# Another table for the order of all operations, and ten corrected costs of the plan, in a one-core attention and feed-forward kernel

## The chip, the core and the metric

The kernel runs on one core of a Trainium2 chip. The metric is the device time of one execution in microseconds (us); lower is better. A core has five engines that work side by side and meet through semaphores: PE (TensorE: matrix products into PSUM), DVE (VectorE), ACT (ScalarE), POOL (GpSimd) and SP (SyncE, which here issues every DMA). Each engine takes its instructions strictly in the order in which the program holds them, so an instruction that waits holds up all that stand behind it on the same engine.

## The reference

Inputs are `q`, `k`, `v` of 8 batches x 8 heads x 576 tokens x 64, a threshold `tau`, and the weights `w_in` (512 x 2048) and `w_out` (2048 x 512), all wanted in float32 precision.

```python
scores = (q @ k.transpose(0, 1, 3, 2)) / 8
thresh = scores.max(-1) - tau
scores = where(scores >= thresh, scores, -1e9)
attn   = exp(scores - scores.max(-1));  attn /= attn.sum(-1) + 1e-9
x      = heads joined(attn @ v)                  # 4608 tokens x 512
h      = x @ w_in
g      = where(h >= 1, h, where(h <= -1, 0, (h + 1)**2 / 4))
out    = g @ w_out                               # 4608 x 512
```

## The kernel before

Products run in float16 with each number split in a high and a low part (three products instead of one); the scores of batch 0 alone run in float32. The work is cut into 4921 operations, each an engine, an assumed cost in us, and a function that issues its instructions.

- **Weights.** 16 tiles of `w_in` and 16 of `w_out` are loaded (line 792), joined from their two halves (ACT L806 and L815, POOL L813, DVE L821 and L823), squared and summed on PE (`gram`, L834) to find a scale (`w_scale`: DVE L741, PE L744, DVE L481 to L483 and L749), then scaled and split in two parts (POOL L878 to L890, ACT L876 and L882, DVE `rest2` L893, or on PE `diff` L896/L897 and `scaled` L906).
- **q and k** of batch 0 are loaded straight into the tiles `qq` and `kk` (`load32`, L572). Those of later batches go to `raw` (L588), are squared (ACT L594), summed on PE (`sums`, L602, three or four very small products), turned into a scale (DVE `pow2` L481 to L483 and `scales` L610), and split (DVE L634 among others). **v** is loaded to `raw` (L658).
- **Attention.** A tile is 128 query rows of a head. PE makes the scores (`qk32` L1015 for batch 0, `qk` L1026 after that) into one of two PSUM buffers `s`; DVE takes the largest (L1078; for some tiles it copies the scores to a `raw` buffer as well and so frees `s` at once), ACT the exponential (L1087), DVE masks and sums (L1104, or L1091 from a `raw` copy, L1131 for a few), a reciprocal (L1112 or L1116), POOL scales (L1119), ACT and POOL split (L1125, L1128), SP transposes by DMA (L1144), and PE multiplies with v (`av`, L1245). ACT L1253 and DVE L1257 write the result into the buffers `x`.
- **Feed-forward.** `ffn1` (PE L1336) multiplies an `x` block with `w_in`; ACT L1342 and L1345, DVE L1349, ACT L1353 and DVE L1357 make the two parts of g; `ffn2` (PE L1379) multiplies with `w_out` into `acc`; ACT L1397 moves it to `ob`, SP stores it (L1404).

What sets the order: `Plan.order()` goes through the operations in the order of the table `ORDER` (lines 38 to 234, 4921 numbers), gives each a buffer and a start by the assumed costs, sorts all operations by that start, and issues them in that sequence. So the table and the costs together fix the order on every engine and which buffer each operation takes; the instructions themselves are the same for any table.

```python
for o in (self.ops[n] for n in ORDER):
    t = max(o.t, idle[o.eng], dma - self.QUEUE if o.eng == "SP" else 0.0)
    ...
return sorted((self.ops[n] for n in ORDER), key=lambda o: o.t)
```

Of the kernel before, what the change touches and what calls it, by code (L numbers as in the profile page):

```python
# [369 lines left out]
def attn_ffn_kernel(ctx: ExitStack, tc: tile.TileContext, qT, kT, vT, tau, w_in, w_out, out):  # L370
# [7 lines left out]
    B, H, D, S = qT.shape  # L378
# [134 lines left out]
    def tau_consts():  # L513
        V.tensor_scalar(tcs[:, 0:1], tau_sb, 0.0, 2.0 ** -51, ALU.is_ge, ALU.mult)
        V.tensor_scalar(tcs[:, 2:3], tau_sb, 0.0, None, ALU.max)
        V.tensor_scalar(tcs[:, 3:4], tau_sb, 0.0, -(D ** -0.5), ALU.is_ge, ALU.mult)

    c_op = plan.op("POOL", 5.7, consts)
    plan.op("ACT", 0.49, warm_up, [c_op])
    t_ld = plan.op("SP", 0.45, lambda: Y.dma_start(tau_sb, tau.broadcast_to([P, 1])), work=LOAD)  # L520
    t_op = plan.op("DVE", 0.56, tau_consts, [t_ld])
# [919 lines left out]
```

## Time and profile before

| | |
|---|---|
| three timed runs | 1104.99, 1105.64, 1106.31 us; median 1105.64 |
| profiled execution, first to last instruction | 1103.6 us (its time by the clock of the timed runs isn't given) |
| PE busy | 1064.5 us (96%), 9825 matmuls |
| DVE busy | 866.3 us (78%) |
| ACT busy | 840.9 us (76%) |
| POOL busy | 778.9 us (71%) |
| mean granted PE clock | 0.987 |

Busy shares are means over the whole span. In the page's 40 slices of 27.6 us, PE's busy tenths read 6, 7, 6, 8 and then 9 to the end, while DVE reads 6 and then 9 in the next five. A wait that the profile names is the idle time of an engine just before an instruction and what ended it.

### The profile page before, as it was taken

The page shows a single profiled execution, that of the slowest core. Times are in us where ns is not written, and L with a number is a line of the kernel's source. Part 1 is how long each engine was busy: PE and PEld are TensorE (multiplying, and loading weights), DVE is VectorE, ACT ScalarE, POOL GpSimd, SP SyncE. Part 2 cuts the span into 40 slices and gives each one's busy share as a digit, 9 for nine tenths or more (in the row PEclk, how much of TensorE's full clock was granted, in tenths as well). Part 3 has the DMA queues.
Part 4 walks back from the last instruction along what each step waited for, and adds up shares of the span by engine and source line. Part 5 has one row for each costly group of instructions (what it writes and reads, how often), then busy time and mean ns, then how long its engine had stood idle before and what let it go on. Part 6 is the DMA issues. An engine that isn't in the chain of part 4 may idle for free.

```text
span 1103.6 us, 26734 instructions
## 1 busy us (share of the span) xinstructions
PE 1064.5 (96%) x9825; PEld 716.7 (65%) x9825; DVE 866.3 (78%) x2379; ACT 840.9 (76%) x1522; POOL 778.9 (71%) x951
## 2 busy tenths in 40 slices
PE   6768899999999999999999999999999999999998
PEld 4557547665776666766666676766676666666674
DVE  6999998888888888888788787778687788876432
ACT  6888769798887787878778778877777787676443
POOL 6899998779878897778667677777666667466000
PEclk9799999999999999999999999999999999999999
DMA  9996688778985986587856776786657657645300
GB/s 330 303 289 117 136 158 163 122 143 162 184 136 113 174 154 122 121 176 146 164 107 108 152 154 124 129 146 124 146 91 130 138 113 127 118 80 113 72 1 29
DMA packets 419316, 154.91 MB, mean 140 GB/s; under 512 B 398193, under 2 KB 398193, under 8 KB 419185
## 3 DMA queue, kind: packets, MB, share of 16 engines
q1 hardware_dynamic: 419184, 153.21, 68.5%
q8 instruction: 77, 1.26, 0.5%
q14 instruction: 55, 0.44, 0.1%
HBM read 45.09 MB, written 9.44 MB: 49 GB/s over the span
## 4 chain that ended last, share of the span: by engine, by line
PE 80%; DVE 4%; POOL 2%; ACT 1%; issue 1%; DVEq 0%; POOLq 0%; ACTq 0%
PE ph L1336 31%; PE acc L1379 31%; PE s L1026 9%; PE ph L1245 9%; DVE e L1104 1%; DVE s L1078 1%; POOL e L1119 1%; ACT e L1087 0%; POOL hl L1128 0%; DVE kk L634 0%; DVE halves L1357 0%; DVE halves L893 0%; DVE vb L690 0%; DVE e L1091 0%; DVE qq L634 0%
## 5 line engine op out<-in xcount | busy, mean ns | idle before, releaser
L1128 POOL TENSOR_TENSOR hl<-e,hl 128x576 f16<-128x576 f32 x280 | 362.3, 1299 | 89.9 <-ACT hl L1125 81.1
L1336 PE MATMUL ph<-x,halves 128*128 128x256 f16 (+1 forms) x4032 | 400.0, 258 | 3.5 <-DVE halves L821 1.8
L1379 PE MATMUL acc<-halves 128*128 128x512 f16 x1728 | 398.0, 379 | 1.6 <-DVE halves L912 1.5
L1336 PEld LDWEIGHTS <-halves 128*128 128x128 f16 x4032 | 345.0, 98 | 62.5 <-issue 17.6
L1379 PEld LDWEIGHTS <-halves 128*128 128x128 f16 x1728 | 161.1, 98 | 189.3 <-issue 19.1
L1119 POOL TENSOR_SCALAR e<-e,sm 128x576 f32<-128x576 f32 x280 | 221.5, 797 | 70.6 <-DVE sm L1112 53.4
L1087 ACT ACTIVATE e<-s,sm 128x576 f32<-128x576 f32 x273 | 198.4, 739 | 87.9 <-DVE s L1078 67.3
L1078 DVE TENSOR_SCALAR_CACHE_REDUCE s<-s,pc 128x576 f32<-128x576 f32 x252 | 199.0, 821 | 80.2 <-PE s L1026 79.8
L1104 DVE SCALAR_TENSOR_TENSOR e<-s,sm,e 128x578 f32<-128x578 f32 x265 | 212.7, 815 | 38.5 <-ACT e L1087 22.0
L1125 ACT ACTIVATE hl<-e 128x576 f16<-128x576 f32 x280 | 187.8, 679 | 39.2 <-POOL e L1119 29.9
L1342 ACT ACTIVATE asq<-ph,fcs 128x512 f32<-128x512 f32 (+1 forms) x160 | 115.5, 734 | 44.7 <-PE ph L1336 42.4
L1349 DVE SCALAR_TENSOR_TENSOR ph<-ph,fcs,asq 128x512 f32<-128x512 f32 (+1 forms) x160 | 111.6, 699 | 42.0 <-ACT asq L1345 41.0
L1357 DVE SCALAR_TENSOR_TENSOR halves<-ph,fcs,halves 128x512 f16<-128x512 f32 (+1 forms) x192 | 112.8, 610 | 18.3 <-ACT halves L1353 17.6
L1245 PE MATMUL ph<-eT,vst 128*64 128x320 f16 (+2 forms) x1928 | 123.5, 283 | 2.5 <-DVE halves L1357 1.4
L1353 ACT ACTIVATE halves<-ph,fcs 128x512 f16<-128x512 f32 (+1 forms) x192 | 104.9, 578 | 26.6 <-DVE ph L1349 26.0
L1245 PEld LDWEIGHTS <-vst 128*64 128x64 f16 x1928 | 100.2, 112 | 29.2 <-issue 20.2
L1026 PE MATMUL s<-kk,qq 64*128 64x288 f16 (+1 forms) x1680 | 115.8, 285 | 0.8 <-DVE e L1104 0.6
L1026 PEld LDWEIGHTS <-qq 64*128 64x128 f16 (+1 forms) x1680 | 65.7, 96 | 50.0 <-issue 36.1
L1345 ACT ACTIVATE asq<-asq 128x512 f32<-128x512 f32 x144 | 90.0, 628 | 2.5
L1081 POOL TENSOR_SCALAR sm<-sm,tcs 128x2 f32<-128x2 f32 x85 | 25.0, 294 | 51.3 <-DVE s L1078 39.7
L1015 PE MATMUL s<-kk,qq 64*128 64x288 f32 (+1 forms) x160 | 42.3, 519 | 11.0 <-DMA qq<-in_q_dram 6.1
L1257 DVE SCALAR_TENSOR_TENSOR x<-ph,x 128x256 f16<-128x256 f32 (+1 forms) x100 | 31.1, 341 | 15.6 <-ACT x L1253 15.6
(162 smaller groups left out, 837.9 us busy)
## 6 DMA issues: line engine op xcount, KB each, us to landing
raw<-in_v_dram SPq DMA_DIRECT2D x32, 288.0 KB, 3.5
halves<-in_moe_w_in_dram SPq DMA_DIRECT2D x16, 512.0 KB, 7.6
out_dram<-ob SPq DMA_DIRECT2D x32, 256.0 KB, 2.9
raw<-in_q_dram SPq DMA_DIRECT2D x28, 288.0 KB, 3.4
raw<-in_k_dram SPq DMA_DIRECT2D x28, 288.0 KB, 3.5
x<-in_moe_w_out_dram SPq DMA_DIRECT2D x10, 512.0 KB, 5.7
eT<-hl SPq DMA_TRANSPOSE x287, 3.4
halves<-in_moe_w_out_dram SPq DMA_DIRECT2D x4, 512.0 KB, 4.4
```

What stands on the lines that cost most here:

```text
L1026: T.matmul(ap(s, s_ps)[r, f, :SH], ap(qb, qq)[h, ql, c : c + r.stop - r.start], ap(kb, kk)[h, kl, f * SH : (f + 1) * SH], start=ql == kl = ...
L1078: V.tensor_scalar(rows(how, k), sv(k), c, None, ALU.mult, ALU.min, accum_out=col(0, k))
L1087: A.activation(ev(k), rows(how, k), AF.Exp, bias=col(0, k), scale=-1.0)
L1104: V.scalar_tensor_tensor(ev(k, SH + 1), sv(k, SH + 1), col(1, k), ev(k, SH + 1), ALU.is_le, ALU.mult, accum_out=col(2, k))
L1119: G.tensor_scalar(ev(k), ev(k), col(3, k), ESC, ALU.mult, ALU.mult)
L1125: A.activation(part2(k, 0), ev(k), AF.Copy)
L1128: G.tensor_tensor(part2(k, w), ev(k), part2(k, 0), ALU.subtract)
L1245: T.matmul(o[hd * D : (hd + 1) * D, :n], vt[:, k, hd * D : (hd + 1) * D], t[:, kb, x * n : (x + 1) * n], start=m == 0, stop=m == len(block ...
L1336: T.matmul(h[:, i], WTh["i"][:, at_(u), wl * 512 + c * P : wl * 512 + (c + 1) * P], x[:, cc, xl, c0 : c0 + n].rearrange("p (t n) -> p t n" ...
L1342: A.activation(tv()[:, :, c], hv()[:, :, c], AF.Relu, bias=fcs[:, b, q, 0 : 1], scale=fcs[:, b, q, 1 : 2])
L1357: V.scalar_tensor_tensor(both(1)[:, h, :, c], halved(hv)[:, h, :, c], fcs[:, b, q, 3 : 4], both(0)[:, h, :, c], ALU.mult, ALU.subtract)
L1379: T.matmul(ap(ab, accs), gv(h, gl)[:, x], WTh["o"][:, at_(fc + i), wl * 512 : (wl + 1) * 512], start=fc + i == 0 and m == 0, stop=not left ...
```

## The change

The table `ORDER` is replaced by another permutation of the same 4921 numbers, and ten lines that give an operation's assumed cost get other numbers. No function that issues an instruction is changed. Two lines of the table and the costs:

```diff
 ORDER = [
-    2, 3, 5, 4, 869, 870, 872, 569, 0, 571, 579, 570, 572, 871, 7, 574, 873, 874, 581, 584, 951, 580, 575, 961, 875, 576, 6, 16, 952, 586, 859, 589,
...
-    t_op = plan.op("DVE", 0.56, tau_consts, [t_ld])
+    t_op = plan.op("DVE", 0.25, tau_consts, [t_ld])
...
-        ps = plan.op("PE", 0.08, sums, [sq, sk], take=[sb], uses=[cb])
+        ps = plan.op("PE", 0.1, sums, [sq, sk], take=[sb], uses=[cb])
...
-        so = plan.op("DVE", 0.56, scales, [ps, t_op], uses=[cb, sb])
+        so = plan.op("DVE", 0.59, scales, [ps, t_op], uses=[cb, sb])
...
-                thr = [plan.op("DVE", 0.15, partial(sthr, k), [os[k]], uses=[m]) for k in range(n2)]
+                thr = [plan.op("DVE", 0.125, partial(sthr, k), [os[k]], uses=[m]) for k in range(n2)]
...
-                    n = [plan.op("DVE", 0.785, partial(smask, k), [exps[k], thr[k]], uses=[ss[k], m, ee[k]]) for k in range(n2)]
-                    n = [plan.op("DVE", 0.085, partial(sden, k), [n[k]], uses=[m]) for k in range(n2)]
+                    n = [plan.op("DVE", 0.746, partial(smask, k), [exps[k], thr[k]], uses=[ss[k], m, ee[k]]) for k in range(n2)]
+                    n = [plan.op("DVE", 0.075, partial(sden, k), [n[k]], uses=[m]) for k in range(n2)]
...
-                    o = plan.op("ACT", 0.58, partial(shi, k), [o], take=[xx[k]], uses=[ee[k]])
+                    o = plan.op("ACT", 0.575, partial(shi, k), [o], take=[xx[k]], uses=[ee[k]])
...
-            o = plan.op("ACT", 0.665 + 0.235 * (m - 1), relu, [o] + [fscale[b] for b in bs], take=[tb], uses=[hb])
+            o = plan.op("ACT", 0.68 + 0.3 * (m - 1), relu, [o] + [fscale[b] for b in bs], take=[tb], uses=[hb])
...
-            o = plan.op("ACT", 0.65 + 0.353 * (m - 1), ghi, [o], take=[qs[0]], uses=[hb, qs[1]])
-            o = plan.op("DVE", 0.70 + 0.346 * (m - 1), glo, [o], uses=[hb, *qs])
+            o = plan.op("ACT", 0.58 + 0.423 * (m - 1), ghi, [o], take=[qs[0]], uses=[hb, qs[1]])
+            o = plan.op("DVE", 0.663 + 0.38 * (m - 1), glo, [o], uses=[hb, *qs])
```

On every engine most operations move by a few places. Of PE's 711 operations 284 keep their place, and none moves by more than 13. Three places follow, each as it stood and as it stands now; a row is line, instruction, output<-inputs and size.

**The first loads, on SP.** `kk0` and `qq0` are k and q of the first pair of heads in batch 0, `kk1` and `qq1` of the second, `raw` holds v, `halves` the weights. Before:

```order
L520 DMA tau_sb_129<-in_tau_dram 128x1
L572 DMA kk0_75<-in_k_dram 128x576
L572 DMA qq0_79<-in_q_dram 128x576
L792 DMA halves_67<-in_moe_w_in_dram 128x1024 x2
L572 DMA kk1_76<-in_k_dram 128x576
L792 DMA halves_67<-in_moe_w_in_dram 128x1024 x2
L572 DMA qq1_80<-in_q_dram 128x576
L658 DMA raw2_70<-in_v_dram 128x576
```

Now:

```order
L572 DMA qq0_79<-in_q_dram 128x576
L572 DMA kk0_75<-in_k_dram 128x576
L520 DMA tau_sb_129<-in_tau_dram 128x1
L792 DMA halves_67<-in_moe_w_in_dram 128x1024 x4
L658 DMA raw2_70<-in_v_dram 128x576
L572 DMA qq1_80<-in_q_dram 128x576
L572 DMA kk1_76<-in_k_dram 128x576
```

The first pair's loads come one issue earlier, `tau` two later, and the second pair's k and q come last, behind one more load of 288 KB.

**The first work of DVE.** `raw` or `s` as output of L1078 is the maximum of a tile, L821 joins a weight tile. Before, up to the first tile that needs the second pair (the row with `s_61,sm_115`):

```order
L1078 TENSOR_SCALAR raw_68,sm_112<-s_61,tcs 128x576
L1084 TENSOR_SCALAR sm_112<-sm_112,tcs 128x1
L821 SCALAR_TENSOR_TENSOR halves<-ph_63,halves 128x512
L1091 SCALAR_TENSOR_TENSOR e_88,sm_112<-raw_68,sm_112,e_88 128x576
L1115 TENSOR_SCALAR sm_112<-sm_112 128x1
L1116 RECIPROCAL sm_112<-sm_112 128x1
L1078 TENSOR_SCALAR raw_69,sm_113<-s_61,tcs 128x576
L1078 TENSOR_SCALAR raw_71,sm_114<-s_62,tcs 128x576
L821 SCALAR_TENSOR_TENSOR halves<-ph_64,halves 128x512
L821 SCALAR_TENSOR_TENSOR halves<-ph_65,halves 128x512
L1084 TENSOR_SCALAR sm_113<-sm_113,tcs 128x1
L1078 TENSOR_SCALAR s_61,sm_115<-s_61,tcs 128x2x288
```

Now, up to the same tile (the row with `s_62,sm_115`):

```order
L1078 TENSOR_SCALAR raw_68,sm_112<-s_61,tcs 128x576
L1084 TENSOR_SCALAR sm_112<-sm_112,tcs 128x1
L1078 TENSOR_SCALAR raw_69,sm_113<-s_62,tcs 128x576
L1091 SCALAR_TENSOR_TENSOR e_88,sm_112<-raw_68,sm_112,e_88 128x576
L1115 TENSOR_SCALAR sm_112<-sm_112 128x1
L1116 RECIPROCAL sm_112<-sm_112 128x1
L821 SCALAR_TENSOR_TENSOR halves<-ph_65,halves 128x512
L1078 TENSOR_SCALAR raw_71,sm_114<-s_61,tcs 128x576
L1084 TENSOR_SCALAR sm_114<-sm_114,tcs 128x1
L1078 TENSOR_SCALAR s_62,sm_115<-s_62,tcs 128x2x288
```

One L821 instead of three stands ahead of that tile. The two others (the second and third weight tiles) come seven and eight rows behind it.

**PE at the first `diff` of `w_out`, some 121 us into the execution.** Before:

```order
L1379 MATMUL acc<-halves 128x512
L896 MATMUL ph_63<-halves,dgw_124 128x512
L897 LDWEIGHTS minus
L897 MATMUL ph_63<-halves,minus 128x512
L602 LDWEIGHTS sel
L602 MATMUL ph_64<-pc_107,sel 128x2
```

Now:

```order
L1379 MATMUL acc<-halves 128x512
L602 LDWEIGHTS sel
L602 MATMUL ph_64<-pc_107,sel 128x2
...
L896 MATMUL ph_63<-halves,dgw_124 128x512
L897 LDWEIGHTS minus
L897 MATMUL ph_63<-halves,minus 128x512
```

The small sums of a q and k scale now go ahead of the `diff` instead of behind it. On DVE, which reads those sums in L481, the next rows were (before):

```order
L481 TENSOR_SCALAR ph_64<-ph_64 128x6
L482 TENSOR_SCALAR ph_64<-ph_64 128x6
L483 TENSOR_SCALAR pc_107<-ph_64 128x6
L610 TENSOR_SCALAR pc_107<-ph_64 128x6
L1084 TENSOR_SCALAR sm_114<-sm_114,tcs 128x1
L1112 RECIPROCAL sm_117<-sm_117 128x1
L1084 TENSOR_SCALAR sm_116<-sm_116,tcs 128x1
L1078 TENSOR_SCALAR raw_68,sm_113<-s_61,tcs 128x576
L1131 SCALAR_TENSOR_TENSOR s_62,sm_114<-s_62,sm_114,e_91 128x2x288
```

and are now:

```order
L481 TENSOR_SCALAR ph_64<-ph_64 128x6
L482 TENSOR_SCALAR ph_64<-ph_64 128x6
L483 TENSOR_SCALAR pc_107<-ph_64 128x6
L610 TENSOR_SCALAR pc_107<-ph_64 128x6
L1115 TENSOR_SCALAR sm_114<-sm_114 128x1
L1116 RECIPROCAL sm_114<-sm_114 128x1
L985 TENSOR_SCALAR scs<-scs,wsc_o 128x1
L1131 SCALAR_TENSOR_TENSOR s_61,sm_112<-s_61,sm_112,e_89 128x2x288
L1078 TENSOR_SCALAR raw_74,sm_117<-s_62,tcs 128x576
```

The mask L1131 has changed places with the maximum L1078 that waits for the next scores.

## Rows read from the trace of the kernel before

**Rows 1.** Windows: stretch, length, busy us (x instructions) per engine, PEclk, DMA share, GB/s.

```profile
180.00:1100.00 920.00, 917.68 (x8460) 615.01 (x8458) 703.93 (x1921) 699.65 (x1266) 620.57 (x741) 1.00 0.66 125
```

**Rows 2.** Windows: the same columns, 9 to 168 us.

```profile
9.00:168.00 159.00, 132.57 (x1246) 90.86 (x1247) 150.33 (x433) 128.17 (x238) 141.22 (x157) 0.91 0.87 221
```

**Rows 3.** Timeline, 160 to 174 us, DVE and PE: start, us, engine, line, instruction.

```profile
166.42 0.56 DVE L1257 SCALAR_TENSOR_TENSOR x<-ph,x 128x256 f16<-128x256 f32 x2 [0.28 <-ACT x L1253]
166.89 0.15 DVE L1112 RECIPROCAL sm<-sm 128x1 f32<-128x1 f32 x1
166.97 0.19 DVE L985 TENSOR_SCALAR scs<-scs,wsc_o 128x1 f32<-128x1 f32 x1
...
167.01 5.42 PE L1336 MATMUL ph<-x,halves 128*128 128x256 f16 x48
```

**Rows 4.** Timeline, the first 16 us, SP, PE and DVE.

```profile
0.73 0.41 SPq L520 DMA_DIRECT2D tau_sb<-in_tau_dram  x1
...
4.82 0.46 SPq L572 DMA_DIRECT2D qq<-in_q_dram  x1
6.05 2.25 PE L1015 MATMUL s<-kk,qq 64*128 64x288 f32 x6 [6.05 <-DMA qq<-in_q_dram]
8.35 0.82 DVE L1078 TENSOR_SCALAR_CACHE_REDUCE raw<-s,tcs 128x576 f32<-128x576 f32 x1 [4.29 <-PE s L1015]
13.03 1.28 DVE L821 SCALAR_TENSOR_TENSOR halves<-ph,halves 128x512 uint32<-128x512 uint32 x2
14.75 0.83 DVE L1078 TENSOR_SCALAR_CACHE_REDUCE s<-s,tcs 128x576 f32<-128x576 f32 x1 [0.32 <-PE s L1015]
```

**Rows 5.** DMA of the first 20 us: GB/s in 40 slices; tile qq's loads to landing.

```profile
GB/s 0 0 0 0 42 60 51 272 373 411 414 401 328 229 254 293 364 419 426 414 426 439 405 386 400 421 408 417 383 407 387 386 422 399 401 410 418 426 410 418
DMA to landing us min/median/max: 4.3/8.0/8.5
```

**Rows 6.** Waits of DVE, 20 to 100 us: us in total, times, longest.

```profile
DVE halves L823 <- ACT ph L815: 0.5, 1, 0.5
DVE s L1078 <- PE s L1015: 0.4, 1, 0.4
...
DVE halves L823 <- ACT hl L1125: 0.3, 1, 0.3
```

**Rows 7.** Timeline, 118 to 126 us, ACT, PE and DVE.

```profile
119.20 0.19 ACT L594 ACTIVATION_READ_ACCUMULATOR junk<-raw 128x1 f32 x1
121.45 2.04 PE L896 MATMUL ph<-halves,dgw 128*128 128x512 f32 x2 [2.08 <-POOL dgw L764]
123.71 0.26 PE L602 MATMUL ph<-pc,sel 128*128 128x2 bf16 x3
124.01 0.17 DVE L481 TENSOR_SCALAR ph<-ph 128x6 f32<-128x6 f32 x1 [1.07 <-PE ph L602]
125.63 0.82 DVE L1078 TENSOR_SCALAR_CACHE_REDUCE raw<-s,tcs 128x576 f32<-128x576 f32 x1 [0.67 <-PE s L1015]
```

**Rows 8.** Chain of waits, merged: start, us, engine and line, count of matmuls.

```profile
194.75 2.70 PE acc L1379 x12
...
1088.46 10.38 PE acc L1379 x48
```

**Rows 9.** Groups of instructions, 9 to 168 us: count | busy us, mean ns | idle before.

```profile
L1091 DVE SCALAR_TENSOR_TENSOR e<-raw,sm,e 128x576 f32<-128x576 f32 x15 | 16.0, 1071 | 0.5 <-ACT e L1087 0.4
L893 DVE SCALAR_TENSOR_TENSOR halves<-halves,wsc_i 128x512 f16<-128x512 f32 x8 | 9.0, 1139 | 0.0
L893 DVE SCALAR_TENSOR_TENSOR halves<-halves,wsc_o 128x512 f16<-128x512 f32 x8 | 8.1, 1016 | 0.0
```

**Rows 10.** Lines L893 and L1091, whole span: duration ns min/median/max, first and last start.

```profile
L893 DVE SCALAR_TENSOR_TENSOR halves<-halves,wsc_i x8: 742/863/1890, 39.0 to 89.0; 128x512 f16<-128x512 f32 x8
L1091 DVE SCALAR_TENSOR_TENSOR e<-raw,sm,e x15: 801/903/1701, 10.0 to 152.8; 128x576 f32<-128x576 f32 x15
```

**Rows 11.** Timeline, around 18 us, DVE.

```profile
18.20 0.27 DVE L741 TENSOR_REDUCE ssq_i<-acc 128x1 f32<-128x128 f32 x1
```

More of the change, by code (lines that the diff above doesn't have):

```diff
@@ L516, in tau_consts @@
         V.tensor_scalar(tcs[:, 3:4], tau_sb, 0.0, -(D ** -0.5), ALU.is_ge, ALU.mult)
-    c_op = plan.op("POOL", 5.7, consts)
+    c_op = plan.op("POOL", 6.9, consts)
     plan.op("ACT", 0.49, warm_up, [c_op])
     t_ld = plan.op("SP", 0.45, lambda: Y.dma_start(tau_sb, tau.broadcast_to([P, 1])), work=LOAD)
-    t_op = plan.op("DVE", 0.56, tau_consts, [t_ld])
+    t_op = plan.op("DVE", 0.25, tau_consts, [t_ld])
     def order_of(b, p):
```

405 rows, old and new, of tables (ORDER, TILE) are left out of this document.

## The prediction, as put on record before the change was run

> **What bounds the kernel now.** I read the windows first. From 180 to 1100 us PE is busy 917.68 of 920.00 us [rows 1]: 2.3 us of idle time in five sixths of the run, at a granted clock of 1.00, the upper of PE's two levels (2.4 GHz). The order can give back nothing worth naming there; it can only break something. The change issues the same matmuls, so what remains is how late PE gets to this state, plus the few us at the end.
>
> The second view is therefore the window from 9 to 168 us [rows 2]. PE is busy 132.57 of 159.00 us, DVE 150.33. DVE, not PE, is the bound there: 8.7 us of idle time, against 26.4 for PE and 17.8 for POOL. The timeline at the handover [rows 3] says the same: the first wide `ffn1` starts at 167.01, right after DVE has written the last piece of its `x` block (L1257, 166.42 and 0.56 long). Behind that point PE doesn't wait any more, so a shift of this handover is a shift of the end. The question for every moved instruction is whether DVE gets its work ahead of this point done sooner or later.
>
> **The change part by part.** The sum is made against the profiled span, 1103.6 us. The timed runs' median, 1105.64, stands 2.0 above it; part of that lies outside the first and last instruction, and I carry it over unchanged.
>
> *The ten costs.* They issue nothing. They act only by the sort of the operations, which is in the order already: 0.
>
> *The first loads.* The first pair's k and q now go out ahead of `tau`, whose issue took 0.41 us [rows 4], so the first scores, at 6.05 before, and the first maximum on DVE, at 8.35, come about 0.4 earlier. The second pair's k and q lose: `qq1` was issued at 4.82 and landed at most 8.5 us later [rows 4, 5], so at 13.3; now one more load of 288 KB is ahead of it and of `kk1`, and at the 400 GB/s of these slices [rows 5] that is 0.7 us. Less the 0.4, the pair lands 0.3 later, and the first tile that needs it, whose maximum ran at 14.75 behind a wait for PE [rows 4], runs at 15.0. Ahead of it DVE used to have three L821; now it has one. Two L821 took 1.28 us [rows 4]. So at 15.0 DVE is 1.28 + 0.25 = 1.5 us behind its old progress, having waited instead. That is the upper bound, if DVE never catches up. The lower one is -0.4, if only the earlier start counts. DVE catches up wherever it used to wait for something that isn't itself late: between 20 and 65 us it waited 0.5, 0.4 and 0.3 us for ACT and PE [rows 6], 1.2 together. I take 1.5 - 1.2 = **+0.3**.
>
> *The sums ahead of the `diff`, near 121 us.* PE stood before the `diff` until 121.45 for a POOL instruction, and the small sums behind it ran only at 123.71 [rows 7]. DVE stood 1.07 us for them (L481 at 124.01), and 0.67 us more for the next scores (L1078 at 125.63). The sums' last input on ACT was there at 119.4 [rows 7]. Ahead of the `diff` they run in PE's idle time there, and the first wait is gone. The second stays in part: those scores still stand behind the `diff`, so they come only some 0.2 earlier, but the mask L1131, a full-width instruction of about 0.8 us like the L1078 beside it, now stands ahead of the wait. Bounds: 0, if DVE only waits the same time one instruction later, and -1.74, if both waits go. I take **-1.0**, the first wait alone, since the row shows what ends it.
>
> *DVE's load ahead of the handover.* Up to the L1257 that releases the first wide `ffn1`, the new order has one L985 and one L1112 more; one L634 is exchanged for another. By their rows that is 0.19 + 0.15 [rows 3]: **+0.3**. Bounds 0 and +0.3. Nothing hides it while DVE is the bound.
>
> *Changes of kind on PE.* Each step of PE's sequence from one kind of product to another costs something: 48 `ffn2` matmuls in a row take 10.38 us, 216 ns each; 12 between other kinds take 2.70, 225 each [rows 8], so about 0.1 per change. The sequence now has 351 such changes instead of 348: **+0.3**. Bounds 0 and +0.3.
>
> *The end.* PE's last `ffn1` and the four `ffn2` behind it (48 matmuls in 10.38 us [rows 8]) come in the same places, with two of the four exchanged; the last eviction and store hang on them as before: 0. Either bound is a few tenths: the exchanged ones belong to `ffn1` results that are long done.
>
> *All other moves* (most of 4921 operations, by a few places) lie in the stretch where PE doesn't wait [rows 1], or move DVE's order without changing its load: 0. A wait that they make among PE's 2.3 us would cost its own length; a wait that they remove can give back 2.3 us at most.
>
> Sum: 0.3 - 1.0 + 0.3 + 0.3 = -0.1, a span of 1103.5, and **1105.6 us** by the median. That is no change: this kernel's runs scatter by 1.3 us, and a measurement can tell about 0.2%, 2.2 us (below 1103.4 or above 1107.9).
>
> **One cost that the order deals anew.** In the 9 to 168 us window L893 took 9.0 + 8.1 us for 16 instructions and L1091 16.0 us for 15 [rows 9]; the shortest of each took 742 and 801 ns, the longest 1890 and 1701 [rows 10]. At their shortest the 31 would take 11.9 + 12.0 = 23.9 us, so 9.2 us of DVE's busy time there are really waiting inside an instruction. Both read two SBUF tiles, while POOL is busy 141.22 of 159.00 us [rows 2]. The new order meets other POOL instructions at other moments. I leave this term at 0, because the number of such instructions ahead of the handover is the same and the order, read row by row, shows no sign of fewer meetings; its ends are a third of the 9.2 us either way, 3.1 us, an estimate from the spread between the shortest and the longest.
>
> The Trainium skill, page "SBUF — State Buffer", section "Who interferes with whom", explains such rows: a DVE instruction with two SBUF inputs and a POOL instruction that reads SBUF take one shared port in turn, and whichever issues second is blocked until the first ends. The trace agrees as far as it goes: the longest L893, 1890 ns, is its shortest plus 1.15 us. By that rule issue order alone could move the sum above by anything up to the whole 9.2 us, and it gives the first rival.
>
> **The rivals.**
>
> *DVE meets POOL less often (faster).* If a third of the 9.2 us goes, the handover comes 3.1 us sooner: 1105.6 - 3.1 = **1102.5**. For it: the replay that makes the order knows which operations share POOL's port, and ten of its costs have been corrected. Against it: with POOL busy nine tenths of the stretch there is hardly a gap to fall into. It decides from 2.2 us on, a quarter of the excess. Chance 0.29.
>
> *The first weight scale comes late (slower).* The pushed-back L821 are two of the four that PE's first squared sums need, and L741, which reads them, ran at 18.20 [rows 11]. Now the chain ahead of L741 begins at 15.0 with the late tile; three L821 (0.64 each), two maxima (0.83), two masks (about the same) and six small instructions (0.15 to 0.2) stand up to it [rows 3, 4], some 6 us: 21.1, or 2.9 later. If POOL's splitting of the weights, which starts from it, and all of DVE behind that stay late in full, the start term is +2.9 in place of +0.3, and the time 1105.6 + 2.6 = **1108.2**. For it: POOL is the second busiest engine [rows 2]. Against it: POOL has 17.8 us of idle time to catch up in, and DVE does other work meanwhile. It decides from +2.5 on. Chance 0.23.
>
> *The moves do nothing:* in a stretch where one engine is 95% busy, its load sets the handover, whatever the order. That is the forecast itself, with the small terms cancelling. Chance 0.48, which takes in waits of under 2 us anywhere in the stretch behind 180 us.
>
> **How the numbers follow.** The likeliest case gives 1105.6. The range goes from the first rival to just past the second: 1102.4 to 1108.4, which is also the forecast less and plus three us of DVE's waiting inside instructions; a fifth is left outside. Faster by more than 0.2%: 0.29. Within 0.2%: 0.48. Slower: 0.23.
>
> **What would show it.** In the profile of the change: the first maximum on DVE (L1078) near 7.9 us instead of 8.35; a wait for PE of over 1 us ahead of a maximum at about 15.0; L741 near 21; no wait for L602 ahead of L481 near 123 us; the first wide `ffn1` (48 matmuls of 128x256) between 166 and 168; L893 and L1091 together near 33 us of busy time; and PE busy over 99.5% from 180 to 1100 us. The prediction is wrong in its reasons if the handover stays and the time moves, if PE shows new waits of over 2 us behind 180 us, or if the handover moves by more than 2 us with L893, L1091 and L741 where they were.

## The result, and the profile after

The changed kernel took 1112.86 us (median of four runs, 1112.20 to 1113.41), the kernel before 1105.97 beside it: a ratio of 1.006, 95% interval 1.0046 to 1.0074. It is 6.9 us slower, where no change was forecast and 1108.4 was the end of the range. The profiled span grew by 6.7 us, from 1103.6 to 1110.3.

First the windows that answer to [rows 1] and [rows 2], and the span up to the first wide `ffn1` (169.60 us now, 167.01 before); columns as in [rows 1]. The changed kernel:

```profile
180.00:1100.00 920.00, 917.72 (x8461) 615.22 (x8459) 702.97 (x1926) 701.12 (x1268) 620.37 (x745) 1.00 0.68 126
9.00:168.00 159.00, 128.02 (x1216) 88.76 (x1218) 149.69 (x422) 128.21 (x236) 139.66 (x152) 0.91 0.87 219
0.00:169.60 169.60, 132.14 (x1243) 91.31 (x1244) 152.21 (x432) 130.28 (x239) 145.99 (x192) 0.92 0.86 216
```

The last stretch in the kernel before:

```profile
0.00:167.01 167.01, 133.83 (x1243) 91.17 (x1243) 150.27 (x433) 129.09 (x239) 145.84 (x194) 0.92 0.86 221
```

Two readings. The handover (the start of the first wide `ffn1`) comes 2.6 us later: DVE, with the same number of instructions but one, is busy 1.9 us longer and idle 0.65 longer. PE's clock isn't the cause: the granted clock up to there is 0.92 in both. The other 4.1 us of the span are lost behind the handover. The windows from 180 to 1100 us hide that, 917.72 us of PE against 917.68, because in the kernel before PE's last matmul ends at 1098.82: 1.2 us of that window, and of the 2.3 us of idle time that the prediction read there, lie behind PE's work. From the handover to the end of PE's last matmul, the kernel before and the changed kernel:

```profile
167.01:1098.82 931.81, 930.67 (x8583) 625.55 (x8582) 716.02 (x1948) 711.09 (x1283) 633.03 (x757) 1.00 0.66 126
169.60:1105.57 935.97, 933.69 (x8584) 626.47 (x8582) 712.64 (x1948) 710.75 (x1282) 630.00 (x760) 1.00 0.68 126
```

That is 4.2 us more for the same matmuls, and only 1.1 of them are counted as idle time; 3.0 are counted as busy. Shorter stretches show a part of it (the page's columns, changed kernel; the kernel before has 19.95, 20.00 and 20.00 us of PE there):

```profile
260.00:280.00 20.00, 19.68 (x174) 10.98 (x172) 15.63 (x52) 14.61 (x32) 16.95 (x22) 1.00 0.64 121
400.00:420.00 20.00, 19.39 (x186) 12.53 (x182) 15.02 (x45) 16.16 (x34) 17.38 (x23) 1.00 0.81 152
500.00:520.00 20.00, 19.54 (x164) 11.64 (x159) 14.28 (x45) 15.09 (x28) 16.36 (x22) 1.00 0.87 179
```

and only the starts of matmuls show all of it. The timeline of PE at 269 us, changed kernel:

```profile
268.05 1.47 PE L1379 MATMUL acc<-halves 128*128 128x512 f16 x6
269.45 0.29 PE L1026 MATMUL s<-kk,qq 64*128 64x288 f16 x1
270.04 0.89 PE L1026 MATMUL s<-kk,qq 64*128 64x288 f16 x11 [0.29 <-DVE e L1104]
```

A step of scores (`qk`, 12 matmuls) begins, and its second matmul waits for a buffer that DVE's mask L1104 has to free: 0.59 us from start to start, of which 0.29 is counted as idle. The ends of matmuls in a profile are modelled, so half of such a wait passes for work. The Trainium skill, page "Perfetto Trace Analysis", section "Tensor Engine Instruction (MATMUL, LD_WEIGHTS)", says the same: TensorE's end is computed from the size of the instruction, not observed. The trace agrees: of the 4.2 us of new delay 3.0 stand as busy time of the same matmuls. Taken from start to start, such waits make about 5.4 us behind 180 us in the changed kernel and 1.6 in the kernel before.

The start, timeline of the changed kernel, answering to [rows 4] and [rows 11]:

```profile
0.73 0.40 SPq L572 DMA_DIRECT2D qq<-in_q_dram  x1
1.64 0.43 SPq L520 DMA_DIRECT2D tau_sb<-in_tau_dram  x1
4.39 2.29 PE L1015 MATMUL s<-kk,qq 64*128 64x288 f32 x8 [4.39 <-DMA kk<-in_k_dram]
7.47 0.15 DVE L514 TENSOR_SCALAR tcs<-tau_sb 128x1 f32<-128x1 f32 x1 [7.47 <-DMA tau_sb<-in_tau_dram]
7.88 0.82 DVE L1078 TENSOR_SCALAR_CACHE_REDUCE raw<-s,tcs 128x576 f32<-128x576 f32 x1
8.76 3.27 PE L1015 MATMUL s<-kk,qq 64*128 64x288 f32 x8 [2.08 <-DVE raw L1078]
9.43 0.63 ACT L806 ACTIVATE ph<-halves 128x512 f32<-128x512 f32 x1 [7.43 <-DMA halves<-in_moe_w_in_dram]
...
14.83 0.82 DVE L1078 TENSOR_SCALAR_CACHE_REDUCE s<-s,tcs 128x576 f32<-128x576 f32 x1
15.64 2.25 PE L1015 MATMUL s<-kk,qq 64*128 64x288 f32 x4 [3.61 <-DMA kk<-in_k_dram]
...
20.50 0.28 DVE L741 TENSOR_REDUCE ssq_i<-acc 128x1 f32<-128x128 f32 x1
```

The first maximum is at 7.88 as forecast, but by luck: PE starts the scores 1.7 us earlier, and DVE waits for `tau`, whose 0.5 KB landed 5.8 us after issue (3.0 before); in a second profile of the same order (e12 below) it is at 6.71. The maximum at 14.83 agrees with the forecast by luck too. Its tile, `s_62,sm_115`, which was called the first that needs the second pair, still belongs to the first pair: PE made its scores from 8.76 on, ahead of the wait for the second pair's k that ends at 15.64. DVE didn't wait for PE there. The second pair comes with the next maximum, at 19.47 instead of 16.22. The first weight tile is worked on at 9.43 instead of 7.5, and L741 runs at 20.50 instead of 18.20. The groups of [rows 9] are as heavy as before: L1091 16.9 us for 15, L893 8.4 and 8.2 for 8 each, 33.5 us in all against 33.1 (the sums of these rows and of [rows 9]).

### The profile page after: what moved, and what is told of

It reads as the page before. It is cut to its first block, busy times and chain, and to the rows that moved or that the text cites. A ratio compares the mean times of both kernels' runs of the same rounds, so it can differ in the third digit from the quotient of the medians.

```text
span 1110.3 us, 26719 instructions
## 1 busy us (share of the span) xinstructions
PE 1065.8 (96%) x9825; PEld 717.8 (65%) x9825; DVE 864.8 (78%) x2379; ACT 841.7 (76%) x1522; POOL 776.0 (70%) x951
## 4 chain that ended last, share of the span: by engine, by line
PE 75%; DVE 7%; POOL 6%; DMA 5%; issue 3%; ACT 3%; SPq 0%; POOLq 0%; ACTq 0%; DVEq 0%
PE ph L1336 29%; PE acc L1379 28%; PE s L1026 8%; PE ph L1245 8%; DMA eT<-hl 2%; POOL hl L1128 2%; POOL e L1119 2%; DVE s L1078 1%; DVE e L1104 1%; ACT hl L1125 1%; DMA raw<-in_v_dram 1%; DMA halves<-in_moe_w_in_dram 1%; POOL halves L890 1%; DVE halves L893 1%; ACT e L1087 1%
## 5 line engine op out<-in xcount | busy, mean ns | idle before, releaser
L1078 DVE TENSOR_SCALAR_CACHE_REDUCE s<-s,pc 128x576 f32<-128x576 f32 x252 | 199.4, 821 | 71.5 <-PE s L1026 71.2
L1104 DVE SCALAR_TENSOR_TENSOR e<-s,sm,e 128x578 f32<-128x578 f32 x265 | 212.8, 814 | 45.8 <-ACT e L1087 26.7
L1245 PE MATMUL ph<-eT,vst 128*64 128x320 f16 (+2 forms) x1928 | 124.1, 283 | 8.5 <-DVE halves L821 4.2
L1357 DVE SCALAR_TENSOR_TENSOR halves<-ph,fcs,halves 128x512 f16<-128x512 f32 (+1 forms) x192 | 112.9, 610 | 23.8 <-ACT halves L1353 23.5
L1245 PEld LDWEIGHTS <-vst 128*64 128x64 f16 x1928 | 99.8, 112 | 35.2 <-issue 24.7
L1015 PE MATMUL s<-kk,qq 64*128 64x288 f32 (+1 forms) x160 | 40.0, 500 | 14.6 <-DMA kk<-in_k_dram 8.0
L1253 ACT ACTIVATE x<-ph 128x256 f16<-128x256 f32 (+1 forms) x100 | 28.1, 321 | 25.5 <-PE ph L1245 25.5
```

Source lines behind the costliest of these rows:

```text
L1078: V.tensor_scalar(rows(how, k), sv(k), c, None, ALU.mult, ALU.min, accum_out=col(0, k))
L1104: V.scalar_tensor_tensor(ev(k, SH + 1), sv(k, SH + 1), col(1, k), ev(k, SH + 1), ALU.is_le, ALU.mult, accum_out=col(2, k))
L1245: T.matmul(o[hd * D : (hd + 1) * D, :n], vt[:, k, hd * D : (hd + 1) * D], t[:, kb, x * n : (x + 1) * n], start=m == 0, stop=m == len(block ...
L1357: V.scalar_tensor_tensor(both(1)[:, h, :, c], halved(hv)[:, h, :, c], fcs[:, b, q, 3 : 4], both(0)[:, h, :, c], ALU.mult, ALU.subtract)
```

## The experiments

Differences are ratios to the kernel before, run beside each on the same chip; 0.001 is 1.1 us.

| run | what it is | ratio | 95% interval |
|---|---|---|---|
| | the changed kernel | 1.0060 | 1.0046 to 1.0074 |
| e12_new_again | new table, old costs | 1.0060 | 1.0046 to 1.0073 |
| e8_costs_alone | old table, new costs | 1.0002 | 0.9993 to 1.0011 |
| e1_fill_new | new up to 265 us | 1.0050 | 1.0037 to 1.0063 |
| e2_steady_new | new behind 265 us | 1.0009 | 1.0000 to 1.0017 |
| e9_new_start | new up to 100 us | 1.0029 | 1.0017 to 1.0040 |
| e10_new_middle | new from 100 to 265 us | 1.0016 | 1.0008 to 1.0025 |
| e3_new_tau_first | changed, `tau` first | 1.0046 | 1.0034 to 1.0058 |
| e4_old_tau_third | before, `tau` third | 1.0010 | 1.0001 to 1.0018 |
| e15_start_old_loads | e9, old order of loads | 1.0045 | 1.0032 to 1.0058 |
| e5_new_apart | changed, 16 moves on DVE | 1.0050 | 1.0038 to 1.0063 |
| e6_old_together | before, 12 moves on DVE | 1.0006 | 0.9997 to 1.0015 |
| e11_new_tau_apart | e3 and 12 moves on DVE | 1.0036 | 1.0023 to 1.0048 |
| e17_start_tau_apart | e9, `tau` first, 7 moves | 1.0018 | 1.0009 to 1.0028 |
| e14_old_sums_first | before, sums ahead of `diff` | 1.0002 | 0.9994 to 1.0011 |
| e13_new_qk_later | changed, 8 moves on PE | 1.0128 | 1.0114 to 1.0142 |
| e16_new_all_repairs | e11 and the 8 moves on PE | 1.0113 | 1.0097 to 1.0129 |
| e7_old_apart_tau_act | before, a try to be faster | 1.0003 | 0.9994 to 1.0012 |

**Costs alone, and the same instructions again.** In e8 only the ten numbers differ, in e12 only the table.

```diff
-    t_op = plan.op("DVE", 0.56, tau_consts, [t_ld])
+    t_op = plan.op("DVE", 0.25, tau_consts, [t_ld])
...
```

> The kernel before with the ten new costs and the old table. The order on each engine and every buffer come out as in the kernel before, so by every theory the time is the same; what the ratio and the second profile differ by is the scatter of a measurement, which I put at under 0.1% in the ratio and under 1.5 us in a single profile.

> The new table with the old costs. The order on every engine and the buffers are those of the changed kernel, so the same time, ratio 1.0045 to 1.0075; a second profile of the same instructions. If PE's stalls behind 270 us belong to the order, they come again in the same places (5.4 us in 14 steps, the largest near 414 and 509 us); if they are chance landings of DMAs, others come.

e8 is the kernel before, instruction by instruction, and took its time. Its handover came at 168.04 us, that of e2, with the same instructions up to 265 us, at 166.25, that of the kernel before at 167.01; with the new order 169.60, 169.83 (e12), 169.56 (e1) and 170.61 (e13 below, which changes nothing ahead of 260 us). So a single profile scatters by nearly 2 us, more than I had expected, and the mean shift is 169.9 - 167.1 = 2.8. In e12 the stalls stand at the same places, but not all in the same size, and from the handover to PE's last matmul it took 934.05 us, 1.9 less than the changed kernel's first profile:

```profile
260.00:280.00 20.00, 19.68 (x174) 10.99 (x172) 15.62 (x51) 14.59 (x31) 17.09 (x22) 1.00 0.64 118
400.00:420.00 20.00, 19.95 (x198) 12.88 (x194) 14.99 (x45) 16.95 (x35) 18.02 (x23) 1.00 0.83 142
500.00:520.00 20.00, 19.84 (x167) 12.03 (x165) 15.09 (x45) 15.29 (x29) 16.83 (x24) 1.00 0.84 168
```

The first belongs to the order; the other two are partly chance.

**Which stretch.** The table is cut: a first part from one order, the other operations in the sequence of the other (all with the new costs, which do nothing). A table also deals out the buffers; no run here separates that from the order. For e1, in short:

```diff
-ORDER = new
+ORDER = new[:1368] + [n for n in old if n not in new[:1368]]
```

e2 has old and new exchanged, e9 has 548 in place of 1368, and e10 is old to 548, new to 1368, old behind.

> The new table's first 1368 numbers (the work up to about 265 us), then the remaining operations in the old table's sequence. Theory T (two separate losses: 2.6 us ahead of the handover at 167 us, 4 us in new short stalls of PE behind it): 2 to 4 us over the kernel before, a ratio near 1.0025, the first wide ffn1 near 169.6, and PE losing no more than 1 us against the kernel before from 270 us on. Rival U (one loss: PE comes late to the handover, and the lateness itself makes the later stalls, because the other engines are then out of step): the whole 6.9 us, ratio 1.006. Rival V (all of it behind 265 us matters, the start is caught up): under 1 us.

> The old table's first 1368 numbers, then the rest in the new table's sequence: the counterpart. Theory T: 3.5 to 5 us over the kernel before, ratio near 1.004, the first wide ffn1 at 167.0, and new stalls of PE between 265 and 1000 us, inside steps of the scores (qk). Rival U: under 1 us over the kernel before. Rival V: the whole 6.9 us.

> The new table's first 548 numbers (the work up to about 100 us), then all other operations in the old table's sequence. After the runs so far I hold that the loss comes in pieces: the first 100 us (tau's place, small instructions behind their producers) 1.5 to 2 us, the stretch from 100 to 170 us under 1 us, and the rest in waits for DMAs behind it. So: 1.5 to 3 us over the kernel before, ratio 1.0015 to 1.0025, and PE some 1.5 us behind the kernel before at 100 us. Rival M (the middle, 100 to 265 us, makes the loss, the start is caught up): under 0.7 us.

> The old table's first 548 numbers, then the new table's sequence up to its 1368th number (about 100 to 265 us), then the old one's. By the pieces: 0.5 to 1.5 us over the kernel before, ratio 1.0005 to 1.0015. Rival M: 3 to 5 us, ratio 1.003 to 1.0045.

0.0029 + 0.0016 + 0.0009 = 0.0054: the three pieces add up to the change's 0.0060 within the intervals. The start costs most, 3.2 us, the middle 1.8, the rest 1.0 (with an interval that begins at no change). e9 lies above the range expected for it, e10 just above its own; M falls. T falls: it had put 4 us behind 265 us. e1 lies near U's 1.006, but not by U's mechanism: from the handover to PE's last matmul it took 933.04 us, 1.2 more than the kernel before, and not 4. Its waits of PE from 180 to 1100 us, the longest three (the kernel before has the first and 0.2 of the third):

```profile
PE ph L1245 <- DVE halves L1357: 0.9, 1, 0.9
PE ph L1336 <- DVE x L1257: 0.6, 1, 0.6
PE s L1026 <- DVE e L1104: 0.3, 1, 0.3
```

The lateness of the handover is simply carried to the end. The 0.6 us, at 281 us, come in e1 and e10 and neither in the kernel before nor in the changed one: they belong to the cut. And e1's profiled execution was its fastest (1109.70 us), so that its span shows 3.7 us of a median difference of 5.1.

The start's loss lies ahead of the handover, which came at 170.97 in e9, with 931.24 us from there to PE's last matmul (931.81 before). The middle's lies behind it: e10's handover, 167.56, is among those of the old order, and then PE waits. Two of its waits, the second again that of the cut:

```profile
268.03 0.89 PE L1026 MATMUL s<-kk,qq 64*128 64x288 f16 x11 [0.30 <-DVE e L1104]
279.72 1.47 PE L1336 MATMUL ph<-x,halves 128*128 128x256 f16 x12 [0.56 <-DVE x L1257]
```

So some 0.6 of the middle's 1.8 us isn't the change's own.

**The place of `tau`'s load.** e3 (e4 is the counterpart, `tau` behind `kk0` and `qq0`):

```diff
-        return sorted((self.ops[n] for n in ORDER), key=lambda o: o.t)
+        r = sorted((self.ops[n] for n in ORDER), key=lambda o: o.t); r.insert(0, r.pop(r.index(self.ops[2]))); return r
```

> The changed kernel with one DMA moved: the load of tau issued ahead of the first q and k, as before the change; all other queues as the change has them. Theory T1 (tau's 512 bytes go out as 128 pieces, and behind two big loads they hold up the queue for some 3 us; at the head they cost nothing that is seen): the first PE scores near 6 again, tau there by 4, the first weight tile some 1.5 us earlier than the changed kernel's 9.4, and 1.5 to 2.6 us faster than the changed kernel (ratio to the kernel before 1.004 to 1.005). Rival T2 (the late second pair of k and q, behind four weight loads and one v, costs it): within 0.5 us of the changed kernel, ratio 1.006.

> The kernel before with one DMA moved: the load of tau issued third, behind the first k and q. Theory T1: tau lands near 7.4 instead of 3.8, all later loads come 1 to 1.5 us later, the first maximum stays within 0.6 us of its 8.35, and the time is 1.5 to 2.6 us longer (ratio 1.0015 to 1.0025). Rival T2: within 0.5 us of the kernel before, or up to 0.4 us faster.

Moving this one DMA gave the changed kernel back 0.0014, 1.5 us, as T1 has it, and cost the kernel before 0.0010, 1.1 us. The timeline of e3:

```profile
0.73 0.41 SPq L520 DMA_DIRECT2D tau_sb<-in_tau_dram  x1
3.81 0.15 DVE L514 TENSOR_SCALAR tcs<-tau_sb 128x1 f32<-128x1 f32 x1 [3.81 <-DMA tau_sb<-in_tau_dram]
5.95 2.29 PE L1015 MATMUL s<-kk,qq 64*128 64x288 f32 x8 [5.95 <-DMA kk<-in_k_dram]
7.64 0.63 ACT L806 ACTIVATE ph<-halves 128x512 f32<-128x512 f32 x1 [5.63 <-DMA halves<-in_moe_w_in_dram]
```

The first weight tile comes 1.8 us earlier than in the changed kernel, though `tau` now goes ahead of it as well as of q and k, and L741 runs at 18.9. What `tau` does to the other loads shows in the rate, here of the changed kernel in half-microsecond slices of its first 20 us:

```profile
GB/s 0 0 0 101 217 364 382 124 33 41 82 106 172 270 262 328 369 434 410 410 435 407 401 404 405 423 426 403 393 401 396 411 397 407 409 421 394 397 407 397
```

From 4.0 to 6.0 us, while the 128 pieces of 4 bytes are on their way, it falls to 33 to 106 GB/s. Before, with `tau` at the head, the low stretch came first, 42 to 60 GB/s from 2.0 to 3.5 us [rows 5]. Only the place of the pieces was varied, not their number. In e4 the first weight tile is worked on at 10.18 instead of 7.48, a longer delay than T1 expected, and the time is below T1's range. T2 falls: in e3 PE starts the second pair's scores at 14.08, with their loads as late in the order as the change has them (13.99 before, 15.64 in the changed kernel). The intervals of e3 and of the changed kernel overlap; the two opposite moves together carry the reading.

**All first loads.** e15 is e9 with SP's first ten loads in their old order:

```diff
+        f = [2, 5, 4, 569, 579, 7, 574, 584, 6, 16]; p = sorted(r.index(self.ops[x]) for x in f); [r.__setitem__(i, self.ops[x]) for i, x in zip(p, f)]
```

> The kernel of the new first 100 us (ratio 1.0029) with SP's first ten loads in the order of the kernel before, all other queues as they were there. Theory T1 (only tau's place matters among the loads, some 1.5 us; the nine more small instructions right behind their producers, some 1.3 us, stay): ratio 1.0012 to 1.002. Rival T2 (all of the start's loss is in the loads, the second pair's k and q included): ratio 1.0000 to 1.0007. Rival T3 (the loads hardly matter): ratio 1.0025 to 1.003.

None of the three theories: it got slower, 1.0045 against e9's 1.0029. The waits of DVE in its first 40 us (us, times, longest):

```profile
DVE raw L1078 <- PE s L1015: 4.4, 2, 4.3
DVE tcs L514 <- DMA tau_sb<-in_tau_dram: 3.7, 1, 3.7
DVE halves L821 <- ACT ph L806: 2.0, 1, 2.0
```

`tau` is there at 3.7, but the first join L821 waits 2.0 us for ACT (0.8 in e9): the weights now land in an order in which the new DVE and ACT sequences don't want them. The order of the loads and that of the engines are one thing; half of it put back is worse than none.

**Small instructions behind their producers.** The forecast had counted DVE's instructions, not their neighbours. Two pieces of DVE's timeline; first the changed kernel, where the threshold L1084 stands right behind the maximum whose result it reads:

```profile
20.19 0.14 DVE L1078 DVE_READ_ACCUMULATOR s<-s,tcs 128x1 f32 x1
20.37 0.21 DVE L1084 TENSOR_SCALAR sm<-sm,tcs 128x1 f32<-128x1 f32 x1
20.50 0.28 DVE L741 TENSOR_REDUCE ssq_i<-acc 128x1 f32<-128x128 f32 x1
```

then the kernel before, where a join L821 stands between:

```profile
28.34 0.14 DVE L1078 DVE_READ_ACCUMULATOR s<-s,tcs 128x1 f32 x1
28.34 0.68 DVE L821 SCALAR_TENSOR_TENSOR halves<-ph,halves 128x512 uint32<-128x512 uint32 x1
28.94 0.20 DVE L1084 TENSOR_SCALAR sm<-sm,tcs 128x1 f32<-128x1 f32 x1
29.06 0.14 DVE L1115 TENSOR_SCALAR sm<-sm 128x1 f32<-128x1 f32 x1
```

From the end of what stands ahead to the start of what follows it is 20.50 - 20.33 = 0.17 us behind the producer and 29.06 - 29.02 = 0.04 elsewhere: 0.13 us a place. The order has 17 such places ahead of the handover, against 5 before: 12 x 0.13 = 1.6 us. The Trainium skill, page "VectorE: DVE Perf Modes", section "The DRAIN you can't avoid", says that a value that the next DVE instruction reads needs a semaphore, and that between copies this semaphore costs nothing extra. The case here is another one: between a wide instruction and a small one that reads its result the trace shows 0.13 us.

e5 moves 16 of the 17 one DVE operation down, e6 makes 12 such places in the kernel before, e11 is e3 with 12 of the 17 apart. For e5, `x` goes right behind `y` (16 pairs of numbers):

```diff
+        [r.insert(r.index(self.ops[y]), r.pop(r.index(self.ops[x]))) for x, y in [(954, 961), (956, 572), ..., (1234, 1223)]]
```

> The changed kernel with 16 moves on DVE alone, all ahead of the handover: where a small instruction (the threshold L1084, a reciprocal L1112 or L1115) stands directly behind the wide one that writes its input, it goes one place down, behind the next DVE operation. The changed kernel has 17 such places ahead of the handover, the kernel before 5. Theory D (a small instruction right behind its producer can't overlap it: 214 ns instead of about 121, and some 35 ns of gap): 16 times about 0.13 us, 2.1 us less of DVE's time ahead of the handover, so 1.5 to 2.1 us faster than the changed kernel, ratio to the kernel before near 1.0043, with the first wide ffn1 near 167.6. Rival P (DVE's extra time is waiting at the port shared with POOL, in L690, L893 and L1091, and the small instructions only fill gaps): within 0.5 us of the changed kernel, ratio 1.006.

> The counterpart in the kernel before: the first 12 thresholds L1084 that stand apart from their maximum L1078 are pulled up to stand right behind it; nothing else moves on any engine. Theory D: 12 times 0.13 = 1.6 us longer, ratio 1.001 to 1.0015, the first wide ffn1 near 168.5. Rival P: within 0.5 us of the kernel before.

> The changed kernel with both repairs: tau's load first, and the 12 small instructions behind 20 us apart from their producers (the first four, at the start, where DVE waits anyway, stay). Theory: they add up, some 1.5 us for tau and 1.2 to 1.6 for the 12, so 2.5 to 3 us faster than the changed kernel, ratio to the kernel before near 1.0035. Rival (DVE's small instructions are hidden in its waits): no better than with tau's load alone, ratio 1.0046.

DVE's busy time up to the handover follows the moves. Windows of e5, e6 and e8 (the kernel before again), one line from each:

```profile
0.00:170.72 170.72, 134.14 (x1243) 91.93 (x1243) 149.86 (x434) 129.72 (x239) 145.68 (x192) 0.92 0.84 215
```

```profile
0.00:168.53 168.53, 133.60 (x1244) 89.79 (x1244) 152.05 (x433) 129.31 (x239) 145.97 (x194) 0.91 0.86 219
```

```profile
0.00:168.04 168.04, 137.54 (x1243) 94.30 (x1244) 151.18 (x433) 129.66 (x239) 145.57 (x194) 0.89 0.88 220
```

152.21 in the changed kernel falls to 149.86 in e5; 150.27 and 151.18 in the kernel before become 152.05 in e6. This figure scatters too, from 149.05 (e14) to 151.18 with the old order on DVE and from 151.85 (e12) to 153.71 (e13) with the new one, but e5 and e6 each lie outside the range that they started from. The time follows less; e5 and e6 don't reach theory D's times. In e5 the first moves stand where DVE waits anyway, and its wait for the exponential ahead of L1091 grew from 1.1 to 3.8 us, so the handover, at 170.72, didn't come earlier; e6 cost 0.0006, not told apart from e8's 0.0002. With `tau` first and those first moves left out (e11) the moves are worth 0.0010 over e3, with intervals that overlap by more than half. So the cause is shown in DVE's rows and not in the time; that some 1 us of the change comes from it is an estimate. Both repairs together (e11) give back 0.0024, 2.7 us, and the intervals hardly touch.

e17 puts both repairs into the new start alone:

> The kernel of the new first 100 us (ratio 1.0029) with tau's load first and the seven small instructions between 20 and 100 us that stand right behind their producers moved one place down. If these two make the start's loss: 1.5 us plus 7 x 0.13 = 0.9 us less, ratio 1.0005 to 1.001. If the start's loss sits elsewhere (the order of the weights' loads and joins): 1.002 to 1.003.

It gave back 0.0011 of the start's 0.0029, between the two expectations. About 2 us of the start are left, and no run shows where they come from. The order of the weights' loads and joins, which I had named, isn't shown as their cause: L741, at 18.6, is nearly where it was.

**The sums ahead of the `diff`**, one PE operation of the kernel before moved:

```diff
+        r.insert(r.index(self.ops[823]), r.pop(r.index(self.ops[51])))
```

> The kernel before with one PE operation moved: the small sums near 121 us ahead of the diff, as the change has them. The forecast's term: 1.0 us faster (0 to 1.74), ratio 0.999, and no wait of DVE ahead of L481 near 123 us. Rival (the wait only moves: the diff, the scores behind it and POOL come later by what the sums take, and DVE waits for the scores instead): within 0.3 us, ratio 1.000.

No gain: 1.0002. DVE's waits from 100 to 167 us, kernel before, then e14:

```profile
DVE ph L481 <- PE ph L602: 1.1, 1, 1.1
DVE raw L1078 <- PE s L1015: 0.7, 1, 0.7
```

```profile
DVE raw L1078 <- PE s L1015: 1.8, 1, 1.8
```

The wait for the sums is gone, as forecast, and stands whole ahead of the next maximum: 1.1 + 0.7 = 1.8.

**Steps of scores one place later.** Eight `qk` inside which PE waited go behind the next `ffn1` or `ffn2` (e13); e16 adds this to e11.

```diff
+        [r.insert(r.index(self.ops[y]), r.pop(r.index(self.ops[x]))) for x, y in [(1611, 3899), (1691, 3927), ..., (3481, 4679)]]
```

> The changed kernel with eight moves on PE alone, all behind 260 us: a step of scores (qk) inside which PE waited goes one step down, behind the ffn1 or ffn2 that followed it. Theory S (PE reaches these steps before DVE's masks L1104 have freed the second buffer of scores; one step of feed-forward between covers it): the stalls at these places go (3.3 us in the first profile of the changed kernel, about 2.3 in the second), and the time falls by 1.5 to 3 us, ratio to the kernel before 1.0035 to 1.0045. Rival L (the lateness comes from DMAs that land late, and PE would wait a step later all the same): within 0.5 us of the changed kernel, ratio 1.006.

> The changed kernel with tau's load first, the 12 small instructions apart, and the eight steps of scores one place later. If the three causes are separate and real: 2.7 us (measured for the first two) and 1.5 to 3 us less than the changed kernel, ratio to the kernel before 1.001 to 1.002. If the last eight moves do nothing: 1.0036.

Theory S falls: e13 took 7.5 us more than the changed kernel, and e16, at 1.0113 against e11's 1.0036, was no better. PE's waits from 180 to 1100 us in e13, longest first:

```profile
PE ph L1245 <- DVE halves L1357: 2.3, 1, 2.3
PE acc L1379 <- ACT ob L1397: 2.2, 2, 1.4
PE ph L1336 <- DVE x L1257: 1.5, 1, 1.5
```

In the changed kernel none of these three is there. The first comes like this (DVE, e13):

```profile
307.39 0.83 DVE L1078 TENSOR_SCALAR_CACHE_REDUCE s<-s,pc 128x576 f32<-128x576 f32 x1 [3.71 <-PE s L1026]
...
308.87 0.75 DVE L1357 SCALAR_TENSOR_TENSOR halves<-ph,fcs,halves 128x512 f16<-128x512 f32 x1
```

Scores that come a step later leave DVE with nothing, for 3.7 us here, and what stands behind them on its queue, L1357, comes late for PE's L1245. So a wait of PE inside these steps, 0.6 us from start to start, cost less than the moves that were to avoid it. At 507 us the chain is another one: POOL's L685 waits for the transposes of v (waits of POOL, 495 to 510 us, changed kernel; 1.2 us at the same place in e12, 0.8 in e2):

```profile
POOL vb L685 <- DMA vst<-vb: 1.7, 1, 1.7
```

Why that DMA lands later there, with the same issues ahead of it on SP, stays open, and with it how much of the last 1.0 us is the order and how much chance.

**A try for a faster kernel**: the kernel before with `tau` on ACT's queue (and four of its five small instructions apart).

```diff
-    t_ld = plan.op("SP", 0.45, lambda: Y.dma_start(tau_sb, tau.broadcast_to([P, 1])), work=LOAD)
+    t_ld = plan.op("SP", 0.45, lambda: A.dma_start(tau_sb, tau.broadcast_to([P, 1])), work=LOAD)
```

> A try for a kernel faster than both: the kernel before with tau loaded from ACT's queue instead of SP's, so that k and q of the first pair are the first two loads of SP, and with 4 of its 5 places of theory D taken apart. Theory T1 (tau's pieces hold up the queue that they stand in): k and q land 0.4 to 1.5 us earlier, first scores near 5, and with 4 x 0.13 us on DVE 1 to 2 us faster than the kernel before, ratio 0.998 to 0.999. Rival (tau on another queue holds up the same 16 engines all the same): within 0.5 us, ratio 1.000, or slower if tau, whose constants the first maximum needs, lands behind 7.

1.0003: no gain; the rival held. The first k, issued at 0.73, landed 4.5 us later with `tau` on its way on the other queue; in e4, with `tau` behind it, 2.9 us later. No run beat the kernel before.

## Why the prediction was wrong

*The ten costs: 0.* Right (e8).

*The first loads: +0.3.* This is the step that failed by most, in its path and by size: the first 100 us of the new order are worth 3.2 us (e9, which takes in all their moves). The step followed the second pair's k and q. What it followed came close by luck: the first maximum, at 7.88, waited for `tau`, the one at 14.83 isn't the second pair's, and the wait for PE that was to stand ahead of it isn't there. It left out what `tau`, now behind two large loads, does to the loads behind it: 1.1 to 1.5 us by e3 and e4. It left out the small instructions too, and about 2 us of the start stay without a shown cause (e17). The 1.2 us that DVE was to catch up weren't caught up: from 20 to 65 us it was idle for 1.99 us, 2.12 before. The second rival came nearer in its numbers (L741 at 21.1, the start term at +2.9; they are 20.50 and 3.2), but its path isn't shown: in e17 L741 runs at 18.6, 0.4 late, and 0.0018, 2 us, are still lost.

*The sums ahead of the `diff`: -1.0.* Wrong: 0 (e14). The step took the first wait as gone because the row names what ended it; the next wait on the same queue took it over whole. The lower bound of that very step, "DVE only waits the same time one instruction later", is what happened.

*DVE's load ahead of the handover: +0.3.* Wrong in kind: the load isn't the count of instructions. 12 more small instructions right behind their producers put 1.6 us on DVE; how much of it reached the end isn't told apart from noise (e11 against e3, 1.1 us).

*Three changes of kind on PE: +0.3.* Not tried alone.

*All other moves: 0, because PE doesn't wait behind 180 us.* Wrong. The step read PE's busy time as work. It holds waits inside PE's steps, and of the 2.3 us of idle time beside it 1.2 lay behind PE's last matmul; with the new order the stretch from the handover on took 4.2 us more in the first profile and 2.2 in the second (e12). By time the new order behind 265 us costs 1.0 us (e2, not clear of noise), that of 100 to 265 us 1.8 (e10, 0.6 of it from the cut).

*The port term: 0.* Right: 33.5 against 33.1 us. The first rival, a gain there, is out.

Small terms of both signs were let cancel; in the runs the gain was 0 and the losses added up.

## What to carry to other kernels

Where one engine bounds a stretch, a wait that goes is a gain only if the next wait on the same queue goes too: follow the queue to the next thing that is late. Read a new order pair by pair: a small instruction right behind its producer costs more than the same one a place later. And a matrix engine that the profile shows busy for 933.69 of 935.97 us can still lose time: compare the starts of the same matmuls, not the busy share, and end the window where its work ends. A wait inside a step isn't a fault by itself, since moving the step to avoid it may starve the engine that it feeds. A load of 0.5 KB in many pieces can hold up large ones, so look at the place of the small loads too.

## What was not expected of the hardware

A load of 0.5 KB, 4 bytes for each partition, landed 3.0 us after issue as the first DMA (before; 3.1 in e3), and 4.4 (e9), 5.8 (changed kernel) and 7.2 us (e4) as the third, behind two loads of 288 KB; while it was on its way the others slowed down, on its own queue and, in e7, from another. The Trainium skill, page "DMA: Bandwidth & Descriptors", section "Specifications", names 512 bytes as the least transfer for line rate; no run here varied the size. And the same instructions gave handovers from 166.25 to 168.04 us (at granted PE clocks of 0.92 and 0.89 up to there), so of two kernels that differ by less than that one profile each decides nothing.
